# Attention loads and tail stores issued by GpSimd instead of SP, in a kernel of one attention layer and two feed-forward layers

## Chip, cores and metric

The kernel runs on one core of a Trainium2 chip. The metric is the device time of one execution in microseconds (us). The median of three runs before the change is 1044.53 us. The engines carry short names in the profile: PE is TensorE (PEld its weight loads), DVE is VectorE, ACT is ScalarE, POOL is GpSimd, SP is SyncE. "SPq" marks an instruction of SP's sequencer that issues a DMA.

## What is computed

The inputs are q, k and v of shape (4, 8, 576, 64) (batch, heads, sequence, head width), a decay f of shape (4, 8, 576), and the weights of two feed-forward layers, 512 to 2048 and back.

```python
def _attn_ref(q, k, v, f):
    scores = np.matmul(q, k.transpose(0, 1, 3, 2)) / np.sqrt(D)
    cum = np.cumsum(np.log(np.clip(f, 0.0001, 1.0)), axis=-1)
    decay = cum[:, :, :, None] - cum[:, :, None, :]
    scores = np.where(causal, -1e9, scores + decay)
    attn = np.exp(scores - np.max(scores, axis=-1, keepdims=True))
    attn = attn / (np.sum(attn, axis=-1, keepdims=True) + 1e-09)
    return np.matmul(attn, v)

def reference(...):
    x = attention output as (2304, 512)
    x = (s * np.maximum(x @ w_in, 0) ** 2 + b) @ w_out
    h = x @ w2_in
    return np.maximum(0.01 * h, h) @ w2_out
```

## The kernel before

**Units.** `unit_list` (L31) cuts the work into eight units, numbered from 0. Units 0 to 3 are the first 256 queries of the four batches, units 4 to 7 the other 320 queries (256, and a tail of 64). A ninth round, u = 8, does the first feed-forward layer for the four tails together. Unit 0's attention has code of its own (L546 to L646). For units 1 to 7 the heads are taken in pairs, four pairs to a unit, so pairs 0 to 27; pairs 8 to 27 belong to units 3 to 7.

**Slots.** A pair's scores come in tiles: two for a pair of units 1 to 3 (one per head), five for a pair of units 4 to 7 (two per head, and one tile for the tails of both). A slot (L650) does `st_split` for one tile, `st_av` for the one before, and `st_score` for the next:

- `st_score` (L311): TensorE writes scores into PSUM (L283 to L307), VectorE adds the decays from the tile `cumk` (L327), ScalarE takes the exponential (L345).
- `st_split` (L354): VectorE makes the divisor (L359, L360); for a tail's tile POOL clears a part of the buffer `p_hl` (L369); ScalarE writes the upper half of the probabilities into `p_hl` (L370) and VectorE the rest (L371). `p_hl` has three buffers. SP issues a DMA transpose from `p_hl` to `p_t` (L375).
- `st_av` (L377): TensorE multiplies `p_t` with the transposed values `v_st` (L393); ScalarE and VectorE gather the result in `x_raw` (L412, L413). After a pair's last tile its result is scaled into x (L427, L428), and for units 4 to 7 POOL scales the tail (L423), which L424 stores to `xld` in DRAM.

**Loads.** `load_pair` (L198) brings queries and keys of a pair into `qk_p` (two buffers), two pairs ahead; it is called after the last score of a pair. `load_cumk` (L216) brings the decays of one job (a head, or the tails of a pair, then as two DMAs) into `cumk` (three buffers, L448), three jobs ahead. `load_v` (L205) brings v of the next pair into `v_raw`, a buffer of the pool `wp` that also holds all weights (33 buffers, L71). `split_v` (L236) splits v for the next pair: L240 clears the end of the buffer on POOL, L243 to L251 find a scale on VectorE, POOL does L252 and L255, VectorE L256, and SP issues two transposes into `v_st` (L261).

**First feed-forward layer.** While unit u+1's attention runs in slots, unit u goes through the layer: per block i, TensorE multiplies (L705), ScalarE and VectorE make the activation g in two halves (L727 to L729 and L730), TensorE multiplies on (L749). The result goes to `x1d` in DRAM (L769, L771, issued by SP). `split_w` (L108) makes two halves of each weight block, the second on POOL (L111); weights are loaded by SP. The tails are read back from `xld` by `last_x1` (L430). The second feed-forward layer (L801 to L836) follows from about 600 us on.

**Order.** Each engine works in order. Which order that is, the tile framework plans from a simulated timeline (L960) with priorities (`ahead`, L444). All DMAs of the kernel are issued by SP.

Of the kernel before, what the change touches and what calls it, by code (L numbers as in the profile page):

```python
# [17 lines left out]
P = 128  # L18
# [20 lines left out]
def attention_moe_moe_kernel(  # L39
# [15 lines left out]
    nc = tc.nc  # L55
# [11 lines left out]
    NL = S - 2 * UN  # L67
# [9 lines left out]
    xld = dram.tile([DM, UN], F32, name="xld")  # L77
# [87 lines left out]
    heads = [(u, h) for u in range(1, NU - 1) for h in range(H)]  # L165
# [5 lines left out]
    for j in range(0, len(heads), 2):  # L171
        u, h = heads[j]
# [16 lines left out]
    qk_at = [0]  # L189
# [4 lines left out]
    qk_p, cumk, v_raw, v_st, v_inv = {}, {}, {}, {}, {}  # L194
    s_t, t_t, p_hl, p_t, av_t, sm_t = {}, {}, {}, {}, {}, {}
    xs, x_raw = {}, {}

    def load_pair(p):  # L198
        if p >= NP:
            return  # L200
        n = qk_at[p + 1] - qk_at[p]
        qk_p[p] = ap.tile([P, UN + 2 * NL + S], F32, tag="qk", name="qk_p")
        nc.sync.dma_start(out=qk_p[p][:, :n], in_=qk[:, qk_at[p] : qk_at[p] + n])

    def load_v(p):  # L205
        if p >= NP:
            return
        u, h = heads[2 * p]
        b, u0, un, _ = units[u]
        kend = u0 + un  # L210
        v_raw[2 * p] = wp.tile([P, 2 * DM], F32, tag="w", name="v_raw")
        nc.sync.dma_start(
            out=v_raw[2 * p][:, :kend], in_=vT[b, h : h + 2, :, :kend].rearrange("h d s -> (h d) s")
        )

    def load_cumk(jb):  # L216
        if jb >= len(jobs):
            return
        u, h, j, half = jobs[jb]
        b, u0, un, _ = units[u]  # L220
        kend = u0 + (un if half else UN)
        cumk[jb] = ap.tile([P, S], F32, tag="cumk", name="cumk", bufs=NCUM)
        r = b * H + h
        for e in range(2 if half else 1):
            rows = slice(e * D, (e + 1) * D) if half else slice(0, P)
            nc.sync.dma_start(
                out=cumk[jb][rows, :kend],
                in_=cumd[r + e : r + e + 1, :kend].to_broadcast([rows.stop - rows.start, kend]),
            )
# [36 lines left out]
    def run_on(first):  # L266
        return nullcontext() if first else tc.high_priority(offset=P_RUN)
# [43 lines left out]
    def st_score(i):  # L311
# [26 lines left out]
        if last:  # L338
            load_cumk(jb + NCUM)
        if last_of_pair(jb):  # L340
            load_pair(j // 2 + 2)
# [8 lines left out]
    def last_of_pair(jb):  # L350
        u, h, j, half = jobs[jb]
        return half or (h % 2 == 1 and units[u][2] == UN)
# [24 lines left out]
    def st_av(i):  # L377
        jb, n, ts, last = tiles[i]
        u, h, j, half = jobs[jb]
        b, u0, un, _ = units[u]  # L380
        if half or (n == 0 and h % 2 == 0):
            av_t[j // 2] = ps_a.tile([P, 512], F32, tag="ps_v", name="ps_v", bufs=2)
        av, pt = av_t[j // 2], p_t.pop(i)
        to = 0
        for t in ts:
            q0, m = QT[t]
            nk = -(-(q0 + m) // P)
            at = 0 if half else q0 - u0 + h % 2 * UN
            for e in range(P // m):
                for k in range(nk):  # L390
                    for l in range(2):
                        with run_on(t == ts[0] and e == k == l == 0):
                            nc.tensor.matmul(  # L393
                                av[:, at + e * m : at + (e + 1) * m],
                                v_st[j + e][:, k].rearrange("p l d -> p (l d)"),
                                pt[:, to + l * nk + k, e * m : (e + 1) * m],
                                start=(k == 0 and l == 0),
                                stop=(k == nk - 1 and l == 1),
                            )
            to += 2 * nk  # L400
        if not last:
            return
        pr = h // 2
        if not half and h % 2 == 0:
            x_raw[u] = xp.tile([P, UN + NL], F32, tag="x_raw", name="x_raw", bufs=2)
        xr = x_raw[u]
        at = UN if half else 0
        for e in range(2) if half else [h % 2]:
            own, oth = slice(e * D, (e + 1) * D), slice((1 - e) * D, (2 - e) * D)
            m = NL if half else UN  # L410
            src, o = av[:, e * m : (e + 1) * m], xr[own, at : at + m]
            nc.scalar.copy(o, src[oth])  # L412
            nc.vector.tensor_tensor(out=o, in0=src[own], in1=o, op=ALU.add)  # L413
        if not last_of_pair(jb):
            return
        if pr == 0:
            xs[u] = xp.tile([P, 2, ND, UN], F32R, tag="x", name="x", bufs=2)
        inv = v_inv[j - j % 2][:, 4:5]
        with ahead(P_X):
            split_x1(xs[u], pr, xr[:, :UN], inv)  # L420
            if un > UN:
                xl = xr[:, UN:]
                nc.gpsimd.tensor_scalar(xl, xl, inv, 0.0, ALU.mult, ALU.add)  # L423
                nc.sync.dma_start(out=xld[pr * P : (pr + 1) * P, b * NL : (b + 1) * NL], in_=xl)  # L424

    def split_x1(x, d, raw, inv):
        nc.scalar.mul(x[:, 0, d], raw, inv)  # L427
        nc.vector.scalar_tensor_tensor(x[:, 1, d], raw, inv, x[:, 0, d].bitcast(F32), ALU.mult, ALU.subtract)  # L428
# [15 lines left out]
    def ahead(n):  # L444
        return tc.high_priority(offset=n)
# [16 lines left out]
    def slot_d(i):  # L462
        if 0 <= i - LAG < NTL:
            st_av(i - LAG)

    def slot_b(i):
        if i < NTL:
            jb, n, ts, last = tiles[i]
            st_score(i)
            u, h, j, half = jobs[jb]  # L470
            if n == 0 and h % 2 == 0 and not half:
                load_v(j // 2 + 1)
            if last and h % 2 == 1:
                split_pair_v(j // 2 + 1)
# [29 lines left out]
    for a in range(P // BH):  # L504
# [11 lines left out]
        out=mask_h,  # L516
        in_=mask_h,
# [7 lines left out]
    for e in range(2):  # L525
        nc.gpsimd.affine_select(
            out=mask_l[e * D : (e + 1) * D],
            in_=mask_l[e * D : (e + 1) * D],
# [11 lines left out]
        out=cl[BH : 2 * BH, :S], in0=cum, in1=cl[:BH, :S].bitcast(F32), op=ALU.subtract  # L540
# [81 lines left out]
    for h in range(H + 2):  # L622
        with ahead(P_F):
            if h >= 2:
                first_c(h - 2)
            if 1 <= h <= H:
                first_b(h - 1)
            if h < H:
                first_a(h)
        if h == 3:  # L630
            nc.sync.dma_start(out=sb[:, 0:1], in_=s1.unsqueeze(0).to_broadcast([P, 1]))
            nc.sync.dma_start(out=sb[:, 1:2], in_=b1.unsqueeze(0).to_broadcast([P, 1]))
        for _ in range(W_PACE):
            if len(w1.blocks) < 2 * NF - 5:
                w1.load(nc.sync)
        with ahead(P_W):
            w1.split_to(W_FIRST + W_PACE * h - W_BACK)
        if h == 6:
            load_v(0)
            load_pair(0)  # L640
            load_cumk(0)
            split_pair_v(0)
        if h == 7:
            load_cumk(1)
            load_cumk(2)
            load_pair(1)  # L646
# [317 lines left out]
```

## Time and profile before

| what | before |
|---|---|
| median of three runs (lowest, highest) | 1044.53 us (1044.37, 1044.6) |
| the profiled execution, its own time | 1039.49 us |
| its span, first to last instruction | 1037.7 us |
| TensorE busy, of the span | 986.1 us, 95% |
| VectorE, ScalarE busy | 537.9 us, 521.3 us |
| POOL busy | 151.8 us |
| mean granted TensorE clock | 0.992 |
| DMA moved | 116.68 MB |

The rows of later sections come from this one profiled execution. Times of rows are from the start of its span. The busy time of an engine counts its compute instructions; issuing a DMA is not counted. "Idle before" is the time for which an engine stood still ahead of an instruction, with the releaser that ended most of it. The time to landing of a DMA runs from its issue until the data has arrived.

### The profile page before, as it was taken

Reading aid. Unit: us, or ns where it says so; the run is one execution under the profiler, and the core shown is the slowest. Engines: PE = TensorE matmul, PEld = TensorE weight load, DVE = VectorE, ACT = ScalarE, POOL = GpSimd, SP = SyncE. Lnnn points to the kernel's source line nnn. Section 1 sums busy time; section 2 is a strip of 40 time slices with the busy share of each in tenths; the row PEclk is TensorE's granted clock in tenths of the full one; section 3 lists DMA queues with packets and bytes.
Section 4 is the critical chain, followed back from the end, with each engine's and each line's share of the span. In section 5 each row is a group of like instructions: output and inputs, shape, how many; then the busy total and the mean of one; then the engine's idle time right before and its main releaser. Section 6 shows DMA issues by size and latency. Waiting matters only on the chain.

```text
span 1037.7 us, 18127 instructions
## 1 busy us (share of the span) xinstructions
PE 986.1 (95%) x6664; PEld 851.0 (82%) x6664; DVE 537.9 (52%) x1410; ACT 521.3 (50%) x1283; POOL 151.8 (15%) x234
## 2 busy tenths in 40 slices
PE   7887789989999999999999999999999999999998
PEld 4676679879888888888999998778888888888897
DVE  6899773665667766777531399873111311211111
ACT  4777696655656766677643566552221221221232
POOL 4434424110101010100000135430000000000000
PEclk9899999999999999999999999999999999999999
DMA  8499491566889999989620463701000100100010
GB/s 282 152 245 269 89 211 40 136 134 134 186 155 181 180 179 197 185 170 192 90 83 2 168 239 94 239 13 49 33 1 1 61 1 1 41 0 1 1 41 21
DMA packets 184296, 116.68 MB, mean 112 GB/s; under 512 B 137040, under 2 KB 163152, under 8 KB 184208
## 3 DMA queue, kind: packets, MB, share of 16 engines
q1 hardware_dynamic: 184208, 115.53, 47.0%
q8 instruction: 52, 0.85, 0.3%
q14 instruction: 36, 0.29, 0.1%
HBM read 74.00 MB, written 10.04 MB: 81 GB/s over the span
## 4 chain that ended last, share of the span: by engine, by line
PE 47%; issue 3%; DVE 3%; POOL 2%; DMA 1%; ACT 1%; POOLq 0%; SPq 0%; ACTq 0%; DVEq 0%
PE ps_o L823 17%; PE ps_h L807 16%; PE ps_o L749 6%; PE ps_h L705 6%; POOL w L111 2%; PE ps_v L393 1%; DVE wt L103 1%; DMA w_raw<-in_moe_w_out 1%; DVE wt L105 1%; DVE wt L102 1%; PE ps_s L296 1%; DMA p_t<-p_hl 0%; ACT wt L101 0%; PE ps_s L283 0%; DVE g L730 0%
## 5 line engine op out<-in xcount | busy, mean ns | idle before, releaser
L705 PE MATMUL ps_h<-x,w 128*128 128x256 f32 x1728 | 242.9, 286 | 5.0 <-POOL w L111 3.3
L749 PE MATMUL ps_o<-g,w 128*128 128x256 f32 (+1 forms) x1536 | 226.8, 289 | 10.8 <-ACT g L729 6.3
L705 PEld LDWEIGHTS ps_h<-x,w 128*128 128x128 f32 x1728 | 220.4, 190 | 7.7 <-POOL w L111 3.9
L823 PE MATMUL ps_o<-w,g 128*128 128x512 f32 x864 | 216.1, 396 | 1.8 <-DVE g L815 1.8
L807 PE MATMUL ps_h<-x,w 128*128 128x512 f32 (+1 forms) x960 | 213.6, 370 | 0.0
L749 PEld LDWEIGHTS ps_o<-g,w 128*128 128x128 f32 x1536 | 197.3, 190 | 17.5 <-ACT g L729 7.9
L807 PEld LDWEIGHTS ps_h<-x,w 128*128 128x128 f32 x960 | 169.0, 188 | 34.4
L823 PEld LDWEIGHTS ps_o<-w,g 128*128 128x128 f32 x864 | 160.5, 188 | 41.5 <-DVE g L815 3.5
L815 DVE TENSOR_TENSOR g<-ps_h,g 128x512 fp32r<-128x512 f32 (+1 forms) x80 | 51.0, 637 | 258.3 <-ACT g L814 258.1
L813 ACT ACTIVATE ps_h<-ps_h 128x512 f32<-128x512 f32 (+1 forms) x80 | 43.1, 539 | 250.7 <-PE ps_h L807 250.7
L345 ACT ACTIVATE tt<-tt,sm 128x512 f32<-128x512 f32 (+4 forms) x128 | 76.0, 594 | 46.5 <-DVE sm L327 45.2
L371 DVE SCALAR_TENSOR_TENSOR p_hl<-tt,sm,p_hl 128x512 f16<-128x512 f32 (+4 forms) x128 | 77.5, 619 | 34.3 <-ACT p_hl L370 33.8
L370 ACT ACTIVATE p_hl<-tt,sm 128x512 f16<-128x512 f32 (+4 forms) x128 | 73.2, 595 | 40.2 <-DMA p_t<-p_hl 31.6
L111 POOL TENSOR_TENSOR w<-wt,w 128x512 fp32r<-128x512 f32 x48 | 73.6, 1537 | 98.0 <-ACT w L110 92.2
L730 DVE TENSOR_TENSOR g<-ps_h,g 128x256 fp32r<-128x256 f32 x128 | 53.6, 421 | 60.9 <-ACT g L729 59.6
L393 PE MATMUL ps_v<-p_t,v_st 128*128 128x128 f16 (+1 forms) x912 | 59.7, 211 | 14.7 <-DMA p_t<-p_hl 11.9
L727 ACT ACTIVATE ps_h<-ps_h 128x256 f32<-128x256 f32 x128 | 46.8, 367 | 50.3 <-PE ps_h L705 49.4
L393 PEld LDWEIGHTS <-v_st 128*128 128x128 f16 x912 | 44.3, 98 | 21.4 <-issue 13.2
L327 DVE CUSTOM_DVE_ANT_0 tt<-ps_s,cumk 128x512 f32<-128x512 f32 (+4 forms) x128 | 59.6, 497 | 2.2 <-PE ps_s L287 0.7
L101 ACT ACTIVATE wt<-w_raw 128x512 f32<-128x512 f32 x64 | 42.7, 672 | 28.2 <-POOL w L111 19.8
L729 ACT CAST g<-ps_h 128x256 fp32r<-128x256 f32 x128 | 47.2, 370 | 7.9 <-PE ps_o L749 4.4
L728 ACT ACTIVATE ps_h<-ps_h 128x256 f32<-128x256 f32 x128 | 46.9, 368 | 3.0
(91 smaller groups left out, 859.9 us busy)
## 6 DMA issues: line engine op xcount, KB each, us to landing
w_raw<-in_moe_w_in SPq DMA_DIRECT2D x32, 512.0 KB, 5.3
w_raw<-in_moe_w_out SPq DMA_DIRECT2D x32, 512.0 KB, 5.8
cumk<-cumd SPq DMA_DIRECT2D x32, 256.0 KB, 3.9
qk_p<-in_qk SPq DMA_DIRECT2D x16, 480.0 KB, 4.8
x1d<-x1o SPq DMA_DIRECT2D x36, 128.0 KB, 2.9
cumk<-cumd SPq DMA_DIRECT2D x32, 144.0 KB, 3.1
v_raw<-in_v SPq DMA_DIRECT2D x16, 288.0 KB, 3.3
out<-o SPq DMA_DIRECT2D x18, 256.0 KB, 2.3
```

The costliest lines, as they stand in the source:

```text
L111: nc.gpsimd.tensor_tensor(w[:, 1], x, w[:, 0].bitcast(F32), ALU.subtract)
L327: nc.vector.tensor_tensor_reduce(tt[:, at + k0 : at + k0 + kw], ps[:, c, :kw] if half else ps[:, h % 2, at : at + w], cumk[jb][:, k0 : k0 ...
L345: nc.scalar.activation(e, e, AF.Exp, bias=sm[:, r : r + 1], scale=-1.0, accum_out=sm[:, 2 + r : 3 + r])
L370: nc.scalar.mul(v[:, 0, :w], e, inv)
L371: nc.vector.scalar_tensor_tensor(v[:, 1, :w], e, inv, v[:, 0, :w], ALU.mult, ALU.subtract)
L393: nc.tensor.matmul(av[:, at + e * m : at + (e + 1) * m], v_st[j + e][:, k].rearrange("p l d -> p (l d)"), pt[:, to + l * nk + k, e * m : ( ...
L705: nc.tensor.matmul(ps, wi[:, a, d * P : (d + 1) * P], x[:, c, d], start=(d == 0 and n == 0), stop=(d == ND - 1 and n == 2),)
L730: nc.vector.tensor_tensor(out=g[:, 1, :UN], in0=ps, in1=g[:, 0, :UN].bitcast(F32), op=ALU.subtract)
L749: nc.tensor.matmul(po[d], wo[:, a, d * P : (d + 1) * P], g[:, c], start=(first and n == 0), stop=(last and n == 2),)
L807: nc.tensor.matmul(ps[:, :n], wi[:, a, d * P : (d + 1) * P], x[:, e, d, :n], start=(d == 0 and k == 0), stop=(d == ND - 1 and k == 2),)
L815: nc.vector.tensor_tensor(out=g[:, 1, :n], in0=raw, in1=g[:, 0, :n].bitcast(F32), op=ALU.subtract)
L823: nc.tensor.matmul(po[m], g[:, a, m * P : (m + 1) * P], wo[:, e, :], start=(i == 0 and k == 0), stop=(i == NF - 1 and k == 2),)
```

## The change

From unit 3 on, POOL (`nc.gpsimd`) issues the loads of `qk_p`, `v_raw` and `cumk`; for all units it issues the store to `xld`, which only units 4 to 7 have. SP keeps the loads of units 1 and 2, all weights, the transposes, the stores to `x1d` and the rest. What is computed is unchanged.

```diff
+    def loader(u):
+        return nc.gpsimd if u > 2 else nc.sync
+
     def load_pair(p):
...
-        nc.sync.dma_start(out=qk_p[p][:, :n], in_=qk[:, qk_at[p] : qk_at[p] + n])
+        loader(heads[2 * p][0]).dma_start(out=qk_p[p][:, :n], in_=qk[:, qk_at[p] : qk_at[p] + n])
...
         v_raw[2 * p] = wp.tile([P, 2 * DM], F32, tag="w", name="v_raw")
-        nc.sync.dma_start(
+        loader(u).dma_start(
             out=v_raw[2 * p][:, :kend], in_=vT[b, h : h + 2, :, :kend].rearrange("h d s -> (h d) s")
         )
...
-            nc.sync.dma_start(
+            loader(u).dma_start(
                 out=cumk[jb][rows, :kend],
...
                 nc.gpsimd.tensor_scalar(xl, xl, inv, 0.0, ALU.mult, ALU.add)
-                nc.sync.dma_start(out=xld[pr * P : (pr + 1) * P, b * NL : (b + 1) * NL], in_=xl)
+                nc.gpsimd.dma_start(out=xld[pr * P : (pr + 1) * P, b * NL : (b + 1) * NL], in_=xl)
```

## Rows read from the trace of the kernel before

**Rows 1.** Stages: length, then busy time (instructions) of each engine, clock, DMA share, GB/s.

```profile
core 0: us, PE busy (x) PEld busy (x) DVE busy (x) ACT busy (x) POOL busy (x), PEclk, DMA share, GB/s
130.00:182.00 52.00, 48.33 (x413) 43.98 (x411) 31.02 (x123) 41.84 (x127) 18.69 (x18) 1.00 0.54 126
182.00:240.00 58.00, 53.01 (x444) 48.02 (x443) 36.00 (x113) 32.88 (x86) 7.35 (x17) 0.97 0.63 138
240.00:468.00 228.00, 218.47 (x2000) 192.19 (x1997) 157.25 (x493) 153.56 (x399) 20.79 (x62) 1.00 0.89 175
468.00:600.00 132.00, 132.00 (x1162) 127.30 (x1162) 60.30 (x161) 73.05 (x190) 8.56 (x43) 1.00 0.48 111
```

**Rows 2.** TensorE's groups, 240 to 468 us: busy, mean ns | idle before, releasers.

```profile
L749 PE MATMUL ps_o<-g,w 128*128 128x256 f32 x613 | 93.2, 291 | 5.1 <-ACT g L729 3.9 <-DVE g L730 0.9
...
L393 PE MATMUL ps_v<-p_t,v_st 128*128 128x128 f16 (+1 forms) x582 | 36.4, 209 | 4.1 <-DMA p_t<-p_hl 4.1
```

**Rows 3.** The same view of TensorE, 130 to 240 us.

```profile
L749 PE MATMUL ps_o<-g,w 128*128 128x256 f32 x312 | 47.5, 295 | 4.8 <-ACT g L729 2.4 <-DVE g L730 1.1 <-DVE vs L250 0.6
...
L393 PE MATMUL ps_v<-p_t,v_st 128*128 128x128 f16 (+1 forms) x129 | 9.4, 216 | 1.3 <-DMA p_t<-p_hl 1.0 <-DMA v_st<-v_hl 0.4
```

**Rows 4.** ScalarE's waits, 130 to 240 us: total us, times, longest.

```profile
ACT p_hl L370 <- DMA p_t<-p_hl: 18.8, 10, 4.4
```

**Rows 5.** ScalarE's waits, 240 to 468 us.

```profile
ACT p_hl L370 <- DMA p_t<-p_hl: 12.4, 8, 2.4
```

**Rows 6.** All engines in order of time, 315 to 317.6 us: start, length.

```profile
315.32 0.72 ACT L370 ACTIVATE p_hl<-tt,sm 128x512 f16<-128x512 f32 x1 [2.07 <-DMA p_t<-p_hl]
...
317.17 0.50 PE L749 MATMUL ps_o<-g,w 128*128 128x256 f32 x2 [1.51 <-ACT g L729]
```

**Rows 7.** SP's issues in order of time, around 240, 424 and 466 us.

```profile
240.47 2.63 SPq L375 DMA_TRANSPOSE p_t<-p_hl  x2
...
422.18 0.57 SPq L203 DMA_DIRECT2D qk_p<-in_qk  x1
422.86 1.36 SPq L375 DMA_TRANSPOSE p_t<-p_hl  x1
424.31 0.72 SPq L212 DMA_DIRECT2D v_raw<-in_v  x1
427.00 1.24 SPq L375 DMA_TRANSPOSE p_t<-p_hl  x1
...
466.53 1.24 SPq L375 DMA_TRANSPOSE p_t<-p_hl  x1
```

**Rows 8.** DMA issues, 422.8 to 424.2 us, then 426.9 to 428.3: us to landing.

```profile
p_t<-p_hl SPq DMA_TRANSPOSE x1, 5.0
...
p_t<-p_hl SPq DMA_TRANSPOSE x1, 3.1
```

**Rows 9.** Waits of SP's queue, 240 to 468 us: total us, times, longest.

```profile
SPq L212 <- DVE v_hl L256: 9.1, 8, 3.2
...
SPq L424 <- POOL x_raw L423: 5.4, 7, 1.5
```

**Rows 10.** Issues of four source lines, whole span: count, ns least/median/most, first and last.

```profile
L203 SPq DMA_DIRECT2D qk_p<-in_qk x28: 328/468/1124, 11.6 to 472.0; - x28
...
L212 SPq DMA_DIRECT2D v_raw<-in_v x28: 337/426/1243, 23.8 to 461.1; - x28
...
L226 SPq DMA_DIRECT2D cumk<-cumd x88: 319/456/863, 14.5 to 495.9; - x88
...
L424 SPq DMA_DIRECT2D xld<-x_raw x16: 324/346/957, 243.8 to 519.8; - x16
```

**Rows 11.** POOL's groups, 130 to 468 us, columns as in rows 2.

```profile
L111 POOL TENSOR_TENSOR w<-w_raw,w 128x512 fp32r<-128x512 f32 x15 | 19.7, 1312 | 28.4 <-ACT w L110 28.4
L255 POOL TENSOR_SCALAR v_hl<-v_raw,vs 128x640 f16<-128x640 f32 (+1 forms) x20 | 14.9, 743 | 14.3 <-DMA v_st<-v_hl 9.2 <-DVE p_hl L371 2.2 <-DVE sm L360 1.2
```

**Rows 12.** VectorE's waits, 130 to 240 us: total us, times, longest.

```profile
DVE vs L243 <- DMA v_raw<-in_v: 10.6, 7, 2.6
```

**Rows 13.** VectorE's groups, 130 to 468 us, columns as in rows 2.

```profile
L256 DVE SCALAR_TENSOR_TENSOR v_hl<-v_raw,vs,v_hl 128x640 f16<-128x640 f32 (+1 forms) x20 | 15.6, 781 | 13.1 <-POOL v_hl L255 13.0
```

## Prediction

> **What bounds the kernel now.** I read the busy time by stage first, then what ended TensorE's idle time in the stages in which the moved transfers run, then the waits of the engines behind it, then SP's queue in order of time, and last what POOL does there.
>
> The stages [rows 1] show where anything can be won. From 468 us to 600 us TensorE is busy all 132.00 us. Before that it lacks 52.00 − 48.33 = 3.7 us (130 to 182), 58.00 − 53.01 = 5.0 us (182 to 240) and 228.00 − 218.47 = 9.5 us (240 to 468), 18.2 us together. Whatever idle time goes there moves the full stretch behind it earlier by as much; whatever is added moves it later. So the sum is one of TensorE's idle time from 130 to 468 us.
>
> What ended it: from 240 to 468 us, 4.1 us until a transpose landed (p_t<-p_hl, the input of L393) and 3.9 us until ScalarE had written g (L729) [rows 2]; from 130 to 240 us, 1.0 us and 2.4 us of the same two [rows 3]. The second is mostly the first at one remove. ScalarE works in order and L370 needs a p_hl buffer back, which a transpose frees when it lands: ScalarE lost 18.8 us to that in the early stretch and 12.4 us in the later one [rows 4, 5]. One case in full: L370 sat 2.07 us until a transpose had landed, L729 stood behind it on the same engine, and L749 on TensorE lost 1.51 us waiting for L729 [rows 6]. So **transposes that land late** carry 4.1 + 3.9 + 1.0 + 2.4 = 11.4 us of the 18.2 us.
>
> Why they are late: all transfers stand in SP's one queue. At 422.18 SP issued a qk_p load and at 422.86 a transpose; at 427.00 it issued another, 2 us after the issue of a v load had ended [rows 7]. The first landed after 5.0 us, the second after 3.1 us [rows 8]. From 240 to 468 us I counted 47 runs of transposes on SP, the first at 240.47 and the last at 466.53 [rows 7]; ahead of 35 of them the instruction before is one that the change moves. Moved transfers also hold the queue with waits for buffers: 9.1 us for v_raw and 5.4 us for xld in that stretch [rows 9], with the transposes behind.
>
> **The change, part by part.** Units are numbered from 0, so u > 2 means units 3 to 7, pairs 8 to 27. Moved are 20 loads of qk_p, 20 of v, 72 of cumk (8 for unit 3; 32 whole ones and 32 halves for units 4 to 7) and 16 stores to xld: 128 DMAs. Nothing is added or dropped, and the bytes are the same.
>
> *SP.* By the medians it gets back 20 × 0.468 + 20 × 0.426 + 72 × 0.456 + 16 × 0.346 = 56.2 us of issue time [rows 10], besides the waits above. Neither is won as such; they count where a transpose stood behind. The landing gap is 5.0 − 3.1 = 1.9 us, more than the largest of the waits on TensorE shown above, so a transpose freed from a load in front can clear its wait. Bounds: nothing, if the bytes of the load slow the transpose just the same from another queue, and 11.4 us, if no wait is left. I take half, **−5.7 us**: most transposes stand behind a moved transfer, but x1d stores and other transposes stay ahead of them, and the loads still run beside them. What is late next is VectorE: after ScalarE's g it is VectorE's half of g, L730, that L749 waits for, 0.9 us [rows 2].
>
> *POOL.* The trace has no DMA issued by POOL, so I bound an issue by neighbours: below by SP's 0.35 us for xld [rows 10], above by POOL's longest instruction, L111, 1.31 us. I take 0.74 us, the mean of L255 [rows 11], because it too is a POOL instruction that goes over 128 rows. Then 128 × 0.74 = 95 us join the 18.69 + 7.35 + 20.79 = 46.8 us that POOL is busy from 130 to 468 us [rows 1]: 142 of 338 us, 42%. With 1.31 us it is 64%. There is room, but POOL's small steps wait their turn: L369 (the memset ahead of a tail's L370), L252 and L255 (v's split), L423. From 240 to 468 us there are some 24 of L255 and L369, the two with work close behind them; a turn lost of 0.74/2 = 0.37 us at each is 9 us if all meet an issue, 4 us at 42%. ScalarE's 12.4 us of waits for transposes go with 3.9 us on TensorE [rows 2, 5], about a third, so I count **+1.3 us** (0 to 3).
>
> A load on POOL that waits for a buffer now holds POOL. For v it costs least: L240, which clears the end of the same buffer, waits there today for the same release. For cumk and qk_p the buffer comes free one pair before the load is needed, so lateness itself is covered; those waits pass to POOL, which idles far longer.
>
> *The loop of v.* From 130 to 240 us v is not covered: VectorE waited 7 times for a v load, 10.6 us [rows 12]. The loop runs v_raw load, L243, L250, L255, L256, and back to the load. If the issue takes 0.74 instead of 0.426 us, 7 × 0.3 = 2.2 us are added; at 1.31 us, 6.2 us; were POOL's issue the quicker one, about nothing. TensorE feels part of VectorE's waits; I count **+0.9 us** (0 to 6).
>
> *xld.* The store waits for L423 on its own engine now, which takes 5.4 us of waits off SP [rows 9]. Its reader comes behind the last tail, in a stretch in which TensorE never idles [rows 1]. Nothing.
>
> Sum: −5.7 + 1.3 + 0.9 = **−3.5 us**. The profiled execution took 1039.49 us around a span of 1037.7, so 1036.0 for it. The median of the runs is 1044.53, 5.0 us above it; the same difference gives **1041.0 us**.
>
> **Rivals.** *The same engines, so no gain.* The transposes' 5.0 us may come from the bytes beside them, not from the place in the queue: the DMA share is 0.89 from 240 to 468 us [rows 1]. Against it: the 3.1 us transpose ran in the same busy stretch. Then −5.7 shrinks to about −1.5 and the costs of 2.2 us stay: 1045.2. By the Trainium skill, DMA: Bandwidth & Descriptors, "Issuing engines are not separate DMA queues", transfers from any engine end on the same 16 DMA engines and interleave, and a second issuer saves only issue time; by that rule the time is this rival's, and the rows on the landing speak against it, with one pair of transposes.
>
> *POOL becomes the late one.* In place of a transpose late on SP, L255 and L369 are late on POOL. It decides when an issue with all that holds it takes (338 − 46.8)/128 = 2.3 us: POOL is then full. Short of it, an issue of 1.31 us that also waits out one VectorE step of L256, 0.78 us [rows 13], makes 2.1 us, 93%. Each of the 24 steps then loses about 1.05 us, 25 us, a third of it 8.3 us; the loop of v adds 7 × 1.7 = 12 us to VectorE, of which I count 0.4, 4.8 us. Against a gain of 7 us (POOL delays the loads, so transposes run freer) that is +6: **1050.5 us**. For it: VectorE is busy 157.25 of 228.00 us [rows 1]. Against: no row shows POOL held up by VectorE's work. The Trainium skill, SBUF — State Buffer, "SBUF: two separate sides", says that POOL cannot write the descriptors of its DMAs while VectorE runs an instruction in a two-port mode, and advises SP or ScalarE as issuer; no run here shows it.
>
> *Unit 3's loads behind the weight splits.* From 130 to 182 us POOL still runs L111, which waited 28.4 us in 15 turns for ScalarE [rows 11], 1.9 us each. Loads queued behind it are late by that; four pairs at 1.9 us, half on the path, take the gain: −3.5 + 4 + 3 = +3.5, 1048.0. The order on each engine is planned from a simulated timeline, so the edit also reshuffles other work; this rival stands for that too.
>
> *All of it goes.* If POOL costs nothing and no transpose is late, −11.4: 1033.1.
>
> **How the numbers follow.** About 0.2%, 2.1 us, is what a measurement of this kernel tells from no change. Chances: forecast 0.36, all of it 0.10 (faster 0.46); same engines 0.23 (same); POOL late 0.23 and unit 3's loads 0.08 (slower 0.31). The forecast's own range is 1036 to 1042.4. To hold 8 in 10 the range takes in the slower cases and most of the full gain: 1034.5 to 1052.
>
> **What would show it.** Right: p_t's landing near 3.1 us, L370's waits for it halved, TensorE's idle from 240 to 468 us down from 9.5 to about 6 us, POOL near 42% there. An issue on POOL above 1.3 us, L256 or L370 waiting for POOL, or VectorE waiting longer for v than 10.6 us would show the costs too small. Wrong altogether: landing times unchanged, or TensorE idle moved into 130 to 240 us.

## Result, and the profile after

The kernel became slower. Its median is 1055.09 us (14 runs, 1046.42 to 1064.32) against 1044.94 us for the kernel before on the same chip (14 runs, 1041.19 to 1047.91): ratio 1.0093, 95% interval 1.007 to 1.0116. Ratios leave out executions in the chip's slower state (one here, one of e5, two of e7), medians and ranges do not. The forecast was 1041.0 with a range up to 1052. The profiled execution took 1046.58 us around a span of 1044.8, near the fastest of the 14 (that of the kernel before, 1039.49, lies below all 14 of its own), so its rows understate the loss; the first experiment below profiles the same kernel again, at 1058.48 us. Line numbers after the change are higher by 3 from the loads on (L370 is now L373, L393 L396, L749 L752).

TensorE's stages after the change, as in [rows 1]:

```profile
core 0: us, PE busy (x) PEld busy (x) DVE busy (x) ACT busy (x) POOL busy (x), PEclk, DMA share, GB/s
130.00:182.00 52.00, 48.01 (x390) 44.06 (x386) 31.62 (x118) 39.69 (x121) 25.88 (x33) 0.94 0.52 116
182.00:240.00 58.00, 51.86 (x414) 47.05 (x411) 32.02 (x101) 32.61 (x83) 16.96 (x33) 0.94 0.64 125
240.00:468.00 228.00, 218.86 (x1988) 192.66 (x1987) 158.54 (x492) 152.08 (x393) 68.18 (x145) 0.99 0.91 176
```

TensorE idles 4.0, 6.1 and 9.1 us: 19.2 us, where it was 18.2. So in this execution idle time explains 1 us of the 7.1 by which the span grew. The granted clock covers the rest: 0.94, 0.94 and 0.99 where it was 1.00, 0.97 and 1.00. Length times what is missing to 1.00 gives 3.1 + 3.5 + 2.3 = 8.9 us after and 1.7 us before.

The groups that answer to [rows 2] (first two lines, 240 to 468 us) and [rows 3] (130 to 240 us):

```profile
L752 PE MATMUL ps_o<-g,w 128*128 128x256 f32 x608 | 94.2, 293 | 5.0 <-DVE vs L250 2.0 <-ACT g L732 1.8 <-DVE g L733 0.8
L396 PE MATMUL ps_v<-p_t,v_st 128*128 128x128 f16 (+1 forms) x576 | 35.6, 209 | 4.1 <-DMA p_t<-p_hl 4.1
...
L752 PE MATMUL ps_o<-g,w 128*128 128x256 f32 x306 | 46.5, 294 | 7.3 <-ACT g L732 3.4 <-DVE x1o L768 2.9 <-DVE g L733 0.7
L396 PE MATMUL ps_v<-p_t,v_st 128*128 128x128 f16 x100 | 8.2, 220 | 1.8 <-DMA p_t<-p_hl 0.9 <-DMA v_st<-v_hl 0.8
```

In the late stretch the wait for ScalarE's g has fallen from 3.9 to 1.8 us and that for p_t is still 4.1 us; in the early one 2.9 us for x1o (L768) are new. Behind these stand ScalarE's waits for a free p_hl [rows 4, 5] and VectorE's for v [rows 12], here in that order (130 to 240, 240 to 468, 130 to 240 us):

```profile
ACT p_hl L373 <- DMA p_t<-p_hl: 13.4, 9, 3.0
...
ACT p_hl L373 <- DMA p_t<-p_hl: 13.3, 7, 3.6
...
DVE vs L246 <- DMA v_raw<-in_v: 6.8, 5, 3.3
```

Both waits of ScalarE were to be halved. The first fell from 18.8 to 13.4 us, the second has gone up from 12.4 to 13.3 us. Why, the landings show. First the kernel before, 130 to 468 us (queue: packets, MB, share; issues: count, KB, median us to landing):

```profile
q1 hardware_dynamic: 116359, 53.86, 78.6%
...
p_t<-p_hl SPq DMA_TRANSPOSE x79, 3.9
...
v_st<-v_hl SPq DMA_TRANSPOSE x39, 3.1
xld<-x_raw SPq DMA_DIRECT2D x13, 32.0 KB, 2.3
```

and the same view after the change:

```profile
q1 hardware_dynamic: 99969, 26.73, 49.9%
q0 software_dynamic: 7206, 26.19, 29.8%
...
p_t<-p_hl SPq DMA_TRANSPOSE x78, 4.3
...
v_st<-v_hl SPq DMA_TRANSPOSE x38, 3.9
```

q1 is SP's queue, q0 GpSimd's. **The transposes, now almost alone with the x1d stores on SP's queue, land later**: 4.3 instead of 3.9 us, and 3.9 instead of 3.1 us. The sum of the two queues' shares is what it was (79.7% and 78.6%).

GpSimd's groups from 130 to 468 us, as [rows 11]:

```profile
L229 POOL DMA_DIRECT2D cumk<-cumd x63 | 33.5, 536 | 68.8 <-DVE sm L330 65.4 <-DVE vs L254 1.8 <-issue 1.2
L111 POOL TENSOR_TENSOR w<-w_raw,w 128x512 fp32r<-128x512 f32 x15 | 19.6, 1308 | 12.4 <-ACT w L110 12.4
L258 POOL TENSOR_SCALAR v_hl<-v_raw,vs 128x640 f16<-128x640 f32 (+1 forms) x20 | 15.1, 754 | 10.1 <-DMA v_st<-v_hl 8.4 <-POOL vs L255 0.3 <-DVE vs L254 0.2
L215 POOL DMA_DIRECT2D v_raw<-in_v x20 | 11.7, 586 | 26.7 <-DVE v_hl L259 26.1 <-POOL w L111 0.6
```

An issue takes 0.54 to 0.59 us. Before a load of decays POOL stands still 65.4 us in all, until VectorE has used the buffer that it is to fill.

One case in full, from the second profile of the changed kernel (e1). First SP and POOL, then who waited, in order of time:

```profile
338.30 1.21 SPq L378 DMA_TRANSPOSE p_t<-p_hl  x1
338.56 0.54 POOL L206 DMA_DIRECT2D qk_p<-in_qk  x1 [0.34 <-PE ps_v L396]
339.09 1.05 POOL L229 DMA_DIRECT2D cumk<-cumd  x2
...
348.30 0.72 ACT L373 ACTIVATE p_hl<-tt,sm 128x512 f16<-128x512 f32 x1 [4.32 <-DMA p_t<-p_hl]
...
349.39 0.74 PE L396 MATMUL ps_v<-p_t,v_st 128*128 128x64 f16 x20 [2.27 <-DMA p_t<-p_hl]
```

and the landings of the first three transfers issued in that moment:

```profile
qk_p<-in_qk POOLq DMA_DIRECT2D x1, 480.0 KB, 7.6
cumk<-cumd POOLq DMA_DIRECT2D x1, 144.0 KB, 9.1
p_t<-p_hl SPq DMA_TRANSPOSE x1, 9.9
```

The transpose was issued first and landed after 9.9 us, at 348.20. Three loads from POOL followed it within 1.3 us, and two of them landed before it, at 346.18 and 348.14. In the kernel before, the loads would have stood behind it in SP's queue. ScalarE lost 4.32 us and TensorE 2.27 us.

### The profile page after: what moved, and what is told of

Its sections match the earlier page's. It is cut to its first block, busy times and chain, and to the rows that moved or that the text cites. A ratio compares the mean times of both kernels' runs of the same rounds, so it can differ in the third digit from the quotient of the medians.

```text
span 1044.8 us, 18164 instructions
## 1 busy us (share of the span) xinstructions
PE 995.7 (95%) x6664; PEld 859.3 (82%) x6664; DVE 539.3 (52%) x1410; ACT 521.6 (50%) x1283; POOL 222.8 (21%) x362
## 3 DMA queue, kind: packets, MB, share of 16 engines
q0 software_dynamic: 8064, 28.84, 10.6%
## 4 chain that ended last, share of the span: by engine, by line
PE 43%; issue 4%; DVE 3%; POOL 2%; DMA 1%; ACT 1%; POOLq 0%; DVEq 0%; ACTq 0%
PE ps_o L826 17%; PE ps_h L810 16%; PE ps_o L752 5%; PE ps_h L708 4%; POOL w L111 2%; DVE wt L103 1%; DVE wt L105 1%; DVE wt L102 1%; DMA w_raw<-in_moe_w_out 0%; PE ps_v L396 0%; DMA x1d<-x1o 0%; ACT wt L101 0%; DVE g L733 0%; PE ps_s L286 0%; PE ps_s L299 0%
## 5 line engine op out<-in xcount | busy, mean ns | idle before, releaser
L708 PE MATMUL ps_h<-x,w 128*128 128x256 f32 x1728 | 248.5, 290 | 3.2 <-POOL w L111 1.7
L752 PE MATMUL ps_o<-g,w 128*128 128x256 f32 (+1 forms) x1536 | 228.5, 291 | 14.2 <-ACT g L732 5.5
L708 PEld LDWEIGHTS ps_h<-x,w 128*128 128x128 f32 x1728 | 225.4, 194 | 6.0 <-POOL w L111 2.1
L752 PEld LDWEIGHTS ps_o<-g,w 128*128 128x128 f32 x1536 | 198.4, 191 | 20.6 <-ACT g L732 7.7
L810 PEld LDWEIGHTS ps_h<-x,w 128*128 128x128 f32 x960 | 169.0, 188 | 34.4
L374 DVE SCALAR_TENSOR_TENSOR p_hl<-tt,sm,p_hl 128x512 f16<-128x512 f32 (+4 forms) x128 | 79.9, 640 | 39.4 <-ACT p_hl L373 38.8
L373 ACT ACTIVATE p_hl<-tt,sm 128x512 f16<-128x512 f32 (+4 forms) x128 | 73.4, 595 | 36.2 <-DMA p_t<-p_hl 27.9
L730 ACT ACTIVATE ps_h<-ps_h 128x256 f32<-128x256 f32 x128 | 46.8, 367 | 53.0 <-PE ps_h L708 52.1
L396 PE MATMUL ps_v<-p_t,v_st 128*128 128x128 f16 (+1 forms) x912 | 59.4, 211 | 12.7 <-DMA p_t<-p_hl 9.0
L396 PEld LDWEIGHTS <-v_st 128*128 128x128 f16 x912 | 44.4, 98 | 19.1 <-issue 10.2
L229 POOL DMA_DIRECT2D cumk<-cumd x72 | 38.3, 536 | 84.4 <-DVE sm L330 80.6
```

The source lines that it names most:

```text
L373: nc.scalar.mul(v[:, 0, :w], e, inv)
L374: nc.vector.scalar_tensor_tensor(v[:, 1, :w], e, inv, v[:, 0, :w], ALU.mult, ALU.subtract)
L396: nc.tensor.matmul(av[:, at + e * m : at + (e + 1) * m], v_st[j + e][:, k].rearrange("p l d -> p (l d)"), pt[:, to + l * nk + k, e * m : ( ...
L708: nc.tensor.matmul(ps, wi[:, a, d * P : (d + 1) * P], x[:, c, d], start=(d == 0 and n == 0), stop=(d == ND - 1 and n == 2),)
L752: nc.tensor.matmul(po[d], wo[:, a, d * P : (d + 1) * P], g[:, c], start=(first and n == 0), stop=(last and n == 2),)
L810: nc.tensor.matmul(ps[:, :n], wi[:, a, d * P : (d + 1) * P], x[:, e, d, :n], start=(d == 0 and k == 0), stop=(d == ND - 1 and k == 2),)
```

## Experiments

Each ratio is to the kernel before on the same chip (medians there: 1043.85 for e1 to e4, 1044.79 for e5 to e8, 1044.60 for e9 to e12, 1043.56 for e13 to e16, 1043.83 for e17 and e18).

### e1 to e4: the change again, and its parts alone

e1 is the changed kernel. e2 moves the decays alone, e3 queries, keys and v, e4 the stores to xld; each is the change's diff cut to those lines, as for e4:

```diff
-                nc.sync.dma_start(out=xld[pr * P : (pr + 1) * P, b * NL : (b + 1) * NL], in_=xl)
+                nc.gpsimd.dma_start(out=xld[pr * P : (pr + 1) * P, b * NL : (b + 1) * NL], in_=xl)
```

> The changed kernel unaltered, for a second profile and its spread beside the kernel before on one chip. All theories: 1.007 to 1.012 of before. If the extra time is TensorE running at its lower clock level, the granted clock is again about 0.98 against 0.99 and TensorE's idle time is about equal to before's; if it is idle time behind POOL, the idle time from 130 to 468 us grows by 5 to 10 us.

> Only the cumk loads of units 3 to 7 are issued by POOL (72 of the 128 DMAs, 13.8 MB). Theory A (a load that waits for its buffer at the head of POOL's queue holds up the split of v and the memset behind it; cumk loads waited 80.6 us there): most of the loss stays, +6 to +10 us. Theory B (loads issued by POOL make the transposes land later in proportion to their bytes): half of it, +4 to +5 us. Theory C (another planned order, nothing of the queues): any value, not in step with A or B.

> Only the loads of qk_p and v_raw of units 3 to 7 are issued by POOL (40 DMAs, 13.8 MB, the same bytes as cumk's). Theory A: 0 to +2 us, since these waited only 40 us at POOL's head, 26 us of it for v where POOL had waited before too. Theory B: half of the loss, +4 to +5 us. Theory C: any value.

> Only the 16 stores to xld are issued by POOL. Theories A and B: no change, or 1 to 2 us faster since SP's queue loses 5 to 15 us of waits for L423 ahead of transposes. Theory C: any value within a few us.

Measured: e1 1059.53, ratio 1.0156 (1.0138 to 1.0175). e2 1046.52, 1.003 (1.0009 to 1.0051). e3 1050.0, 1.0062 (1.0046 to 1.0078). e4 1040.71, 0.9976 (0.9959 to 0.9993). So theory A, by which the decays that wait at the head of POOL's queue carry the loss, falls: they cost least. B's signs are met for the loads, its sizes only roughly (2.7 and 6.2 us). The stores gain. By the medians the parts sum to 2.67 + 6.15 − 3.14 = +5.7 us; the whole cost 15.7 on the same chip.

e1 lies above what every theory allowed (1.007 to 1.012), so the same change cost 10 us in one set of runs and 16 in another: differences of a few us between sets tell little. e1's profile, nearer to the median, shows what the first one understated, here its stages and TensorE's wait for p_t from 130 to 468 us:

```profile
130.00:182.00 52.00, 45.80 (x364) 42.43 (x364) 30.36 (x109) 38.60 (x118) 25.70 (x32) 0.90 0.56 120
182.00:240.00 58.00, 52.34 (x415) 47.03 (x413) 33.00 (x109) 33.48 (x86) 16.58 (x31) 0.94 0.54 110
240.00:468.00 228.00, 213.58 (x1920) 187.98 (x1921) 152.79 (x472) 146.89 (x380) 64.81 (x138) 0.99 0.92 170
...
PE ps_v L396 <- DMA p_t<-p_hl: 14.1, 8, 3.2
```

TensorE idles 6.2 + 5.7 + 14.4 = 26.3 us, 8.1 more than in the kernel before, and its wait for p_t is 14.1 us where it was 1.0 + 4.1 [rows 2, 3]. The clock costs 5.2 + 3.5 + 2.3 = 11.0 us by the product above.

In e3, the dearest part, TensorE waits for p_t no longer than before. What grew there are the waits around the split of v: POOL waits 20.5 us for v_st to land (9.2 before [rows 11]) and VectorE 22.7 us for POOL (13.0 before [rows 13]):

```profile
PE ps_v L396 <- DMA p_t<-p_hl: 3.7, 3, 2.3
...
POOL v_hl L258 <- DMA v_st<-v_hl: 20.5, 8, 4.0
...
DVE v_hl L259 <- POOL v_hl L258: 22.7, 12, 4.0
```

### e5 and e6: the queues and the planner's order, apart

Each move also makes the planner order the computing engines anew. These two runs hold an order: a chain of edges, which set the order of issue and no wait, fixes all of TensorE's, ScalarE's and POOL's computing instructions and nearly all of VectorE's (1318 of 1411 by name) as they stand in the other kernel. e5 has the changed queues in the order of before, e6 the queues of before in the changed kernel's order.

```diff
+            tc.add_manual_dep(
+                ins,
+                prev.name,
+                mybir.DependencyInfo(mybir.DependencyClass.NoSync, mybir.DependencyReason.DATA),
+                reason="pin_order",
+            )
```

> The changed kernel's queues (queries, keys, v and decays of units 3 to 7 and all stores of x on GpSimd), with TensorE, ScalarE, VectorE and GpSimd's computing instructions held in the order of the kernel before, so the planner's new order is taken out. Kernel before on the chip of the first four runs: 1043.85; the changed kernel there 1059.5, elsewhere 1055.1. Theory Q (a load on a second queue is served beside the transposes and makes them land later): the loss stays, 1050 to 1060. Theory O (what costs is the new order that the planner gives the computing engines): the loss goes, 1041 to 1046, and the transposes' waits of ScalarE are as before. Half and half would be 1047 to 1050.

> The mirror of the run above: all loads and stores on SP as before, the computing engines in the order of the changed kernel. Theory Q: the time of before, 1042 to 1047. Theory O: slow as the changed kernel, 1051 to 1060. If both orders suit only the queues for which they were planned, both mirrors are slower than before.

Measured: e5 1068.0, 1.0215 (1.0182 to 1.0249); e6 1056.59, 1.0122 (1.0097 to 1.0147). With the queues changed and the order kept, the loss is 23.2 us (22.5 by the ratio), more than in the planner's order: the new order is no cause of it, it takes part of it back. But an order is also good only on the queues for which it was planned. In e6 the v loads come late; VectorE's waits for them from 130 to 468 us, in the kernel before and in e6:

```profile
DVE vs L243 <- DMA v_raw<-in_v: 14.5, 8, 3.8
```

```profile
DVE vs L243 <- DMA v_raw<-in_v: 29.4, 8, 9.5
```

Landings go with the queue in both orders. The table is counted from the traces, over all transposes issued from 130 to 500 us (means in us): from the last write of the buffer to the issue, and from the issue to landing.

| kernel | p_t: to issue | p_t: to landing | v_st: to issue | v_st: to landing |
|---|---|---|---|---|
| before | 1.66 | 4.05 | 6.05 | 3.54 |
| e6, queues of before, changed order | 1.70 | 3.94 | 6.12 | 3.30 |
| changed kernel | 1.48 | 4.66 | 4.99 | 4.30 |
| changed kernel again (e1) | 1.33 | 5.01 | 5.09 | 4.15 |
| e5, changed queues, order of before | 1.68 | 4.81 | 4.73 | 5.37 |
| e2, decays on GpSimd alone | 2.09 | 4.33 | 4.75 | 4.16 |
| e3, queries, keys, v on GpSimd alone | 1.72 | 3.98 | 6.72 | 4.05 |
| e9, loads on ScalarE's queue | 1.35 | 4.39 | 4.47 | 4.94 |
| e10, loads in halves | 1.73 | 4.51 | 4.95 | 4.81 |
| e12, decays on SP | 1.60 | 4.40 | 5.92 | 4.56 |
| e17, before with a fourth p_hl | 1.53 | 4.09 | 5.91 | 3.52 |

A transpose p_t waits for its issue 0.2 to 0.3 us less in the changed kernel (not at all less in e5), and then lands 0.6 to 1.0 us later. For v_st the changed kernel wins 1.0 us ahead of the issue and loses 0.6 to 0.8 behind it. In e3 p_t lands as in the kernel before and v_st 0.5 us later, so the 6.2 us lost there do not come through p_t. In e5 TensorE pays for it at L396, here its waits from 130 to 468 us and its stages:

```profile
PE ps_v L396 <- DMA p_t<-p_hl: 20.9, 6, 7.9
...
PE ps_v L396 <- DMA v_st<-v_hl: 6.7, 2, 4.9
```

```profile
130.00:182.00 52.00, 45.19 (x366) 41.16 (x367) 30.11 (x118) 38.36 (x117) 25.18 (x33) 0.93 0.55 118
182.00:240.00 58.00, 50.24 (x410) 46.04 (x410) 32.50 (x102) 32.65 (x84) 17.52 (x33) 0.94 0.67 116
240.00:468.00 228.00, 200.75 (x1792) 177.68 (x1788) 142.93 (x441) 137.27 (x357) 57.87 (x129) 0.96 0.85 157
```

It idles 6.8 + 7.8 + 27.2 = 41.8 us, and the clock costs 3.6 + 3.5 + 9.1 = 16.2 us by the same product as above: 58.0 us against 18.2 + 1.7 = 19.9 in the kernel before. The difference, 38 us, covers the 33.4 us of the spans (1071.1 and 1037.7).

### e7 and e8: loads that wait, and the early stage

e7 gives the changed kernel one more buffer for decays, e8 leaves unit 3 on SP.

```diff
-        cumk[jb] = ap.tile([P, S], F32, tag="cumk", name="cumk", bufs=NCUM)
+        cumk[jb] = ap.tile([P, S], F32, tag="cumk", name="cumk", bufs=NCUM + 1)
```

```diff
-        return nc.gpsimd if u > 2 else nc.sync
+        return nc.gpsimd if u > 3 else nc.sync
```

> The changed kernel with one buffer more for the decays (bufs=NCUM + 1), so that a load of decays waits less for its buffer at the head of GpSimd's queue (in the changed kernel 84 us of GpSimd's idle time between 130 and 520 us). Theory H (that waiting load holds up the split of v, the memset and the stores behind it): the loss mostly goes, 1044 to 1049. Theories Q and O: the loss stays, 1052 to 1061, with GpSimd's wait for the decays' buffer clearly smaller; under O any time between 1045 and 1060 is possible, as the order changes again.

> The changed kernel with the loads of unit 3 left on SP (u > 3), which are issued while ScalarE and GpSimd still split the weights. Theory U (the loss of some 2 to 7 us at 130 to 200 us comes from unit 3's loads in that stage): 1048 to 1053. Theory Q by bytes (four units of five moved): four fifths of the loss, 1052 to 1056.

Measured: e7 1063.69, 1.0171 (1.0145 to 1.0197); e8 1057.29, 1.011 (1.008 to 1.014). In e7 POOL's wait for that buffer is 56.5 instead of 65.4 us (130 to 468 us), and the time no better. H gets no support, though most of the wait remains, so e12 had to ask it again. U falls: without unit 3's loads the loss is all there. Whether it goes by the bytes can't be told: four fifths of 10 to 16 us are 8 to 13, and the ratio gives 11.5.

### e9 and e10: another issuer, loads in halves

Both start from e5. e9 lets ScalarE issue the loads, e10 cuts each of POOL's loads into two halves of its columns.

```diff
-        return nc.gpsimd if u > 2 else nc.sync
+        return nc.scalar if u > 2 else nc.sync
```

```diff
+    def pieces(u, n):
+        k = 2 if u > 2 else 1
+        at = [n * i // k for i in range(k + 1)]
+        return list(zip(at, at[1:]))
...
-        loader(heads[2 * p][0]).dma_start(out=qk_p[p][:, :n], in_=qk[:, qk_at[p] : qk_at[p] + n])
+        for c0, c1 in pieces(heads[2 * p][0], n):
+            loader(heads[2 * p][0]).dma_start(out=qk_p[p][:, c0:c1], in_=qk[:, qk_at[p] + c0 : qk_at[p] + c1])
```

> The run with the changed queues and the order of before (1068.0, mean landing of the transposes 4.8 us for p_t and 5.4 for v_st, against 4.05 and 3.5 in the kernel before), but with the loads of units 3 to 7 issued by ScalarE instead of GpSimd. Its time is not the point, since ScalarE now spends itself on the issues and on the loads' waits: 1050 to 1110 by every theory. Theory Q2 (any second queue beside SP's delays the transposes): p_t 4.6 to 5.2, v_st 4.6 to 5.8. Theory P (it is the way GpSimd's queue cuts the loads, some 64 packets for each where SP's cuts 128): p_t 3.8 to 4.3, v_st 3.3 to 4.0, and the packets of ScalarE's loads as small as SP's.

> The same as the run with the changed queues and the order of before (1068.0), with each of GpSimd's loads cut into two of half the columns, so packets of half the size and twice the issues (112 more, some 0.55 us each on GpSimd). Theory P (size of the packets that a transpose waits behind): landings fall back to some 4.3 (p_t) and 4.0 (v_st) from 4.8 and 5.4, and the time to 1050 to 1060. Theory Q2: landings as they were or longer, 1065 to 1080.

Measured: e9 1064.67, 1.0175 (1.0128 to 1.0221); e10 1074.83, 1.0289 (1.0259 to 1.0318). The queues of e9 from 130 to 468 us, q10 being ScalarE's:

```profile
q1 hardware_dynamic: 94648, 25.63, 47.3%
q10 hardware_dynamic: 12294, 24.57, 28.7%
```

These counts hold many packets of 4 bytes. Without them, counted from the traces, ScalarE's packets hold 2.3 KB (10746 packets) where POOL's hold 4.8 KB in e5 (4912) and 4.4 KB in e10 (5450). So e10 doubled the issues but hardly made the packets smaller, and of theory P it says nothing. In e9 the transposes land 0.4 us sooner than in e5 (table), about as much as two profiles of one kernel differ (p_t 4.66 and 5.01 in the changed kernel), but v_st stays 1.4 us above the kernel before, and p_t 0.3: p_t between the two theories, v_st as Q2 had it. So a second queue is enough to make them late, whoever issues; that POOL's larger packets add to it is not shown. e10's loss is 30.2 us where e5's was 23.2, with POOL busy 91.42 us from 240 to 468 us instead of 57.87; that the issues are the cause is likely but not shown.

### e11 and e12: the stores alone and the decays back, order held

e11 is e4 in the order of before, e12 is e5 with `nc.sync` again for the decays.

> Only the stores of the tails' x on GpSimd (as in the run that measured 1040.7 against 1043.9), with all computing engines held in the order of before. If that gain came from the queue (SP no longer holds transposes behind a store that waits): 1039 to 1043, ratio 0.995 to 0.999. If it came from the order that the planner gave: 1043.5 to 1047.

> The run with the changed queues and the order of before (1068.0), with the decays back on SP: GpSimd issues queries, keys, v and the stores alone. Theory H (GpSimd stands at loads that wait for the decays' buffer, 68.7 us between 130 and 468, and its computing instructions come late behind them): most of the 23 us goes, 1045 to 1053. Theory Q by bytes (two fifths of the moved bytes are back): 1054 to 1060, landings 4.4 and 4.6.

Measured: e11 1041.05, 0.9973 (0.9953 to 0.9994); e12 1058.68, 1.0121 (1.0089 to 1.0152). The stores' gain is the queue's, not the order's. Without the decays on POOL 14 of e5's 23 us of loss stay, so loads waiting at POOL's head are not most of it: H falls here. Time and landings (4.40 and 4.56 us) are those of Q by bytes.

### e13 to e16: is it the late landing?

e13 is the changed kernel, e14 is e5, e15 is e11, each with a fourth p_hl, so that ScalarE need not wait for the transpose that empties the third. e16 is the kernel before with a spare buffer for decays: a new order and no moved transfer.

```diff
-        ph = ap.tile([P, 10 * P], F16, tag="p_hl", name="p_hl", bufs=3)
+        ph = ap.tile([P, 10 * P], F16, tag="p_hl", name="p_hl", bufs=4)
```

> The changed kernel with a fourth p_hl (bufs=4), so ScalarE writes the next p_hl without waiting for the transpose that empties the last but two (26.7 to 35 us of waits between 130 and 468). If the late landing costs the time by that wait: 1044 to 1050. If it costs by TensorE's own wait for p_t, or if the order does: 1053 to 1062.

> The changed queues with the order of before (1068.0) and a fourth p_hl. Late landing through ScalarE's wait: 1050 to 1060. Through TensorE's own wait for p_t and v_st (29 us there before the matmuls with p_t): 1062 to 1068.

> The best version so far (only the stores on GpSimd, order of before: 1041.05 against 1044.6) with a fourth p_hl. If ScalarE's wait for p_hl (31.2 us between 130 and 468 in the kernel before) costs TensorE there: 1034 to 1039; if it is hidden: 1040 to 1043.

> The kernel before with one buffer more for the decays: no transfer changes its queue, but the planner gives a new order (1862 lines of difference on TensorE). If a new order alone costs some 10 us whatever it is for: 1050 to 1058. If the planner's orders are as good as each other on the queues for which they were made: 1041 to 1047.

Measured: e13 1059.45, 1.0142 (1.0104 to 1.0181); e14 1059.72, 1.0152 (1.0107 to 1.0196); e15 1035.39, 0.9918 (0.9886 to 0.995); e16 1043.31, 0.9998 (0.9973 to 1.0022). e16 shows that a new order alone costs nothing here. In e14 the loss is 16.2 us where e5's was 23.2, so some 7 us of it ran through ScalarE's wait (18.5 us in e5, 8.4 in e14), though the two intervals, taken on two chips, overlap. The matmuls' own waits for p_t and v_st fell too, from 27.6 to 18.4 us, but are still far above the 5.5 of the kernel before. In e13 it brings nothing: in the planner's order other waits take its place (8.2 us for v_st, the longest 7.0).

### e17 and e18: the buffer alone

e17 is the kernel before, its order held, with a fourth p_hl; e18 has the stores on GpSimd and a fourth p_hl, in the planner's order.

> The kernel before, its order held, with a fourth p_hl and no other edit. If the gain of 8 us of the run with stores and fourth p_hl is the sum of the stores' 2.7 and the buffer's 5.5: 1037 to 1040, ratio 0.993 to 0.997. If the buffer needs the stores off SP: 1041 to 1045.

> The stores on GpSimd and a fourth p_hl, in the order that the planner gives to them. If the gain doesn't hang on the held order: 1034 to 1039, ratio 0.990 to 0.995. If the planner's new order gives it back, as it did with the fourth p_hl on the changed kernel: 1040 to 1045.

Measured: e17 1037.51, 0.9942 (0.992 to 0.9964); e18 1036.77, 0.9937 (0.9913 to 0.9962). e17's wait of ScalarE from 130 to 468 us, 31.2 us in the kernel before (18.8 and 12.4 [rows 4, 5]), TensorE's group L749 there, and its stages:

```profile
ACT p_hl L370 <- DMA p_t<-p_hl: 6.9, 3, 3.7
...
L749 PE MATMUL ps_o<-g,w 128*128 128x256 f32 x948 | 141.7, 290 | 7.0 <-ACT g L729 2.8 <-DVE g L730 2.8 <-DVE vs L250 0.5
```

```profile
130.00:182.00 52.00, 48.85 (x422) 45.00 (x422) 31.88 (x125) 43.46 (x131) 19.64 (x18) 0.99 0.53 127
182.00:240.00 58.00, 53.74 (x462) 48.78 (x462) 38.06 (x120) 35.88 (x94) 9.02 (x20) 1.00 0.75 151
240.00:468.00 228.00, 221.39 (x2028) 195.32 (x2027) 158.75 (x496) 153.58 (x397) 20.78 (x60) 1.00 0.88 176
```

TensorE's idle time is 3.1 + 4.3 + 6.6 = 14.0 us instead of 18.2, and of it the wait for ScalarE's g 2.8 us instead of 2.4 + 3.9 [rows 2, 3]. e15, e17 and e18 all beat both kernels; e18 needs two edits and no held order.

## Why the prediction was wrong

**Where to win: right.** Idle time of TensorE from 130 to 468 us, much of it at one remove through ScalarE's wait for p_hl, could be won. The term was 5.7 us of 11.4; e17 won 6.3 us of the median (1043.83 to 1037.51), by a buffer instead of a queue.

**The step that failed** is the one on SP: "a transpose freed from a load in front can clear its wait". It took the gap in landing, 5.0 against 3.1 us [rows 8], for the price of a place in SP's queue. That place is paid before the issue, and there the changed kernel won 0.2 to 0.3 us. The gap lies behind the issue, where the loads under way weigh (in the kernel before, transposes with one under way at their issue took 4.3 us, the others 3.5, counted as below), and there the change made things worse: in one queue a load issued after a transpose stood behind it, in two it runs beside it. Counted from the traces, for the transposes p_t issued from 200 to 500 us: loads of qk_p, v_raw and cumk were issued behind a transpose still on its way 60 times in the kernel before, and none landed ahead of it; in the two profiles of the changed kernel 18 of 102 and 22 of 102 did, in e9 18 of 95. Transposes with such a load issued in their first 2.5 us took 4.0 us in the kernel before and those without 4.2; in the changed kernel 5.0 and 4.5, in e1 5.5 and 4.7. The step had one pair of transposes to go by. Its lower bound, "nothing", was no bound: the effect had the other sign.

**POOL.** The issue was put at 0.74 us, between 0.35 and 1.31; it takes 0.54 to 0.59. POOL is busy 25.9 + 17.0 + 68.2 = 111.0 of 338 us, 33% where 42% was reckoned. That waits for buffers pass to POOL was right (65.4 us), and that they cost little is borne out as far as e7, e12 and e2 go: e7 won nothing back, e12 left 14 of 23 us, and e2, which keeps the waits for the decays' buffer, lost 2.7 us.

**The loop of v**, +0.9: VectorE waited 6.8 us in 5 turns instead of 10.6 in 7 [rows 12]. No cost.

**xld**, counted as nothing: the stores alone win 2.5 us by the ratio of e4 and 2.8 by that of e11. The text had the reason, 5.4 us of SP's waits with transposes behind [rows 9], and did not count it. The store itself lands later from POOL, in 4.7 us in the changed kernel (e1: 5.5) instead of 2.3, without a cost that shows in e4 or e11.

**The rivals.** *Same engines* named the mechanism, that bytes slow a transpose from any queue, and stopped at unchanged landings, 1045.2. The Trainium skill's rule (DMA: Bandwidth & Descriptors, "Issuing engines are not separate DMA queues") says that transfers interleave whoever starts them. The trace agrees with that part (18 times in 102 a load landed ahead of a transpose issued before it), and a second issuer did save a little ahead of the issue; but on it the transposes landed later and the time was 1.0093, which that rule does not say. *POOL becomes the late one* asked for issues of 2.3 us; the longest of all 128 took 0.75 us. The Trainium skill's reason for it (SBUF — State Buffer, "SBUF: two separate sides") finds no trace in the issues: the 72 issues of decays lie between 0.52 and 0.59 us while VectorE is busy 222 of 338 us. *Unit 3's loads and the new order*: e8 and e16 clear both.

**The checks named.** "Wrong altogether: landing times unchanged, or TensorE idle moved into 130 to 240 us": landings grew, and the early idle went from 8.7 to 10.1 us, with a lower clock there.

**What stays open.** How the changed kernel's own 10 to 16 us divide among its waits. Held to the order of before, the queues cost 23 us, 7 of them through ScalarE's p_hl; in the planner's order the same edit wins nothing (e13), and the same order costs 12 us on the queues for which it was not made (e6). That the landing is what the queues do to the transposes is shown; that it is all they do is not. e3, which lost 6.2 us with p_t landing as before, points at v_st for a part; how large a part is open. Why a second queue delays the transposes by as much as it does was not taken further than the order of landings.

## What to carry to other kernels

Before moving transfers off a queue to free a critical one, split its lateness into the part before the issue and the part after: only the first was won here, and the shared queue protected a transfer from what was issued behind it. Where an engine waits for a transfer only to get a buffer back, one more buffer is the cheaper try (here 2.5 KB a partition won 6 us). A planned order fits its own queues; judge a move with the order held and with it free.

## What the runs showed of the hardware

A wait of some 3 us can cost more than its length, since TensorE's clock was low after it. In the changed kernel's profile, TensorE waited 2.88 us ahead of 197.45 us for x1o, which VectorE had been late with because ScalarE waited 2.28 us for p_t; the stretches around it, with the granted clock as the third number from the end:

```profile
194.00:197.40 3.40, 0.56 (x5) 0.36 (x4) 1.73 (x5) 2.24 (x7) 0.32 (x1) 1.00 0.27 74
197.40:198.20 0.80, 0.75 (x2) 0.60 (x3) 0.71 (x3) 0.60 (x2) 0.39 (x2) 0.51 0.30 78
198.20:202.00 3.80, 3.80 (x18) 3.04 (x18) 1.45 (x7) 0.94 (x4) 1.13 (x3) 0.65 0.83 155
202.00:206.00 4.00, 4.00 (x39) 3.95 (x37) 1.26 (x3) 1.11 (x3) 1.07 (x2) 1.00 1.07 246
```

After 3.4 us with 0.56 us of work the clock stood at 0.51, which is the lower of its two levels (1.2 instead of 2.4 GHz), then at 0.65 over the next 3.8 us, and at 1.00 from 202. That is 0.49 × 0.8 + 0.35 × 3.8 = 1.7 us lost behind the wait. In e1 a wait of 3.16 us for p_t ahead of 137.63 us was followed by a longer one:

```profile
137.60:144.00 6.40, 6.37 (x39) 5.81 (x40) 4.41 (x17) 6.33 (x23) 3.14 (x6) 0.51 0.59 144
144.00:150.00 6.00, 6.00 (x58) 5.69 (x57) 4.81 (x20) 3.21 (x11) 2.94 (x6) 1.00 0.93 128
```

Here 0.49 × 6.4 = 3.1 us were lost. So these two waits took half to all of their length again at the lower clock (the wait of 1.51 us in the kernel before [rows 6] took nothing: the clock is 1.00 from 240 to 468 us), and a sum of idle times, as in the prediction, misses that part: 8.9 us in the changed kernel and 11.0 in e1 against 1.7 in the kernel before.
